# Feed-forward weights requested as one group behind a segment's output store, and GpSimd squares issued behind the values matmuls, in a segment-recurrent transformer block

## The chip, the cores and the metric

The kernel runs on one core of a Trainium2 chip. The metric is the device time of one execution in microseconds (us). Profiled executions come with a trace of every instruction and DMA packet. A profile is one execution and can lie a few us beside the median: the profiled run of the kernel before took 1187 us, 10 us over its median. So I take differences of *times* from the timed runs, and use the profiles to say *where* the time is.

## The reference, cut to what matters

```python
# 2048 rows of 640; 64 segments of 32 rows; 8 memory rows carried from segment to segment
for s in range(n_seg):
    h = concat([mem, xs])                  # 40 rows
    q, k, v = h @ Wq, h @ Wk, h @ Wv       # 32 heads of 128
    p = softmax(mask(q k^T * scale))
    o = (p v) @ Wo
    mem = o[:8]                            # the next segment needs this output
h  = x + o_all
h2 = h + relu(layernorm(h) @ w1 + b1)**2 @ w2 + b2     # feed-forward, 1728 wide
```

The recurrence over 64 segments is serial. The feed-forward part is independent work, and the kernel threads it into the recurrence: the feed-forward of one block of 128 rows is spread over four segments of the next blocks.

## The kernel before

One *segment* is one call of `step(b, sp)`, `sp` = 0 to 3. TensorE goes through: the projection passes (`ps`, 120 wide matmuls), the scores (`A`), a share of feed-forward matmuls (`psf` going up, `psy` coming down), the softmax sums (`pz`), more feed-forward, the values matmuls (`O`, 64 small ones), a strip of tail projections, and the output projection (`pw`, 128 small ones). VectorE makes `pn` = p * rz (rz, one over the softmax sums, comes from ScalarE), which the values matmuls wait for.

The feed-forward weights come from HBM in tiles of 320 KB, 14 per block, into five buffers. A tile is requested when its buffer's last matmul has been issued:

```python
def load_wf(n):
    if n < NB * FC:
        t = wfp.tile([128, 1280], BF16, tag="wf", name="wf")      # WB = 5 buffers
        nc.sync.dma_start(out=t[:], in_=wf_d[n % FC])
        wfs[n] = t
...
def run(units, us, early=False):
    while units and us > 0:
        ...
        if early and late and late[0][0]:
            late.pop(0)[1]()          # one ReLU evacuation is pulled ahead of pn
            early = False
...
# in ffn(b), up(k, u):
                if u == 1:
                    wfs.pop(b * FC + k)
                    load_wf(b * FC + k + WB)
                    late.append((1, lambda: evac(k, ps)))

        def evac(k, ps):
            r = s2.tile([128, 2, 128], BF16, tag="r", name="r")
            for u in range(2):
                nc.vector.tensor_scalar(out=r[...], in0=ps[...], ...)          # bias, ReLU
            if k < 6:
                nc.gpsimd.tensor_tensor(out=f1T[...], in0=r[:], in1=r[:], op=ALU.mult)   # square
            ...
# the feed-forward block begins with loads and a layer norm, taken one piece per projection half:
        side.append(loads)                       # x, and o back from HBM, on the Sync queue
        side.extend([lambda: None] * 3)
        side.append(add)                         # GpSimd: h = o + x
        side.extend(norm_steps(...))             # VectorE: statistics, statistics, ...
...
# in step(b, sp):
        run(full, ..., True)                     # second share of feed-forward matmuls
        ...
        nc.vector.tensor_tensor(out=pn[:, 0:MC], in0=p[:, 0:MC], in1=rz[:], op=ALU.mult)
        nc.vector.tensor_tensor(out=pn[:, MC:AC]..., in0=ptail, in1=head16(rz), op=ALU.mult)
        ... values matmuls O, evacuation oT, strip, output projection pw ...
        nc.scalar.copy(out=o[:], in_=pw[:, 0:DG])
        nc.sync.dma_start(out=o_main[b * 4 + sp]..., in_=o[:])
        ...
        run(strip, 1.28 if sp < 3 else 100)
```

After segment 0 the strip ends with the store `o_tail` of the block's last rows. `loads` (in segment 1) reads it back, so the chain `o_tail` store, `fo` load, GpSimd `add`, VectorE statistics runs through the Sync queue.

The softmax here doesn't subtract the row's maximum and nothing guards it: scores larger than these inputs give would overflow.

## Time and profile before

| | before |
|---|---|
| time, median | 1177.3 us (1173.0 to 1182.6, 20 runs) |
| profiled span, granted clock | 1185.4 us, 0.970 |
| PE / VectorE / ScalarE / GpSimd busy | 84 / 40 / 38 / 14 % |
| idle before pw matmuls, put down to "issue" | 73.2 us |
| values matmuls wait for pn | 20.6 + 9.8 us |

From the page of the kernel before: engines, the DMA queue of the instructions (packets, MB, share), the chain that ended last, and the output projection's group (busy us, mean ns | idle us before it, what ended it).

```profile
PE 994.8 (84%) x30400; PEld 727.9 (61%) x30400; DVE 477.0 (40%) x1076; ACT 449.9 (38%) x945; POOL 164.8 (14%) x468
...
q8 instruction: 237, 3.88, 1.3%
...
PE 76%; issue 8%; DMA 6%; DVE 5%; ACT 3%; POOL 1%; SPq 0%; ACTq 0%; DVEq 0%; POOLq 0%
...
L217 PE MATMUL pw<-wo,oT 128*32 128x160 bf16 x8192 | 171.6, 240 | 75.7 <-issue 73.2
```

"issue" means that TensorE waited for nothing that the profile shows. One such wait, in the timeline of TensorE before (start, us, what; in brackets the idle time before it):

```profile
535.15 1.01 PE L217 MATMUL pwt<-wo,oTt 128*32 128x160 bf16 x48
535.99 1.21 PE L217 MATMUL pw<-wo,oT 128*32 128x160 bf16 x58
539.96 1.22 PE L217 MATMUL pw<-wo,oT 128*32 128x160 bf16 x60 [2.77 <-issue]
```

The projection stops after 58 of 128 equal matmuls. Counting the TensorE instructions up to each such stop is what explains it: 49 of the 53 gaps over 0.4 us between 150 and 1095 us begin at remainder 190 modulo 256. The instruction queue q8 moves 237 packets of 16,384 bytes, and 60,800 TensorE instructions (30,400 matmuls and as many weight loads) are 237.5 times 256. So I read these as waits for the next block of 256 instructions. The packet for this stop ran from 537.63 to 538.51 us; the next matmul started 1.45 us after it.

The stretches around that stop, in the table of windows before (us, busy time of each engine, then PEclk, the granted clock, the DMA share and GB/s):

```profile
533.00:537.00 4.00, 3.45 (x186) 3.24 (x183) 3.05 (x10) 1.19 (x3) 2.48 (x9) 1.00 0.85 278
537.20:539.90 2.70, 0.00 (x0) 0.00 (x0) 0.00 (x1) 0.00 (x0) 0.46 (x2) 1.00 0.14 53
541.10:544.50 3.40, 3.35 (x102) 2.89 (x94) 0.34 (x1) 0.34 (x2) 0.00 (x0) 0.50 0.05 12
```

Just before the stop the DMA engines are 85% busy, with weight tiles. And after the stop the clock is 0.50 for 3.4 us.

The timeline before around the same segment's pn (a segment 0), where a square of GpSimd runs beside the small multiply (128x128; the large one is 128x320):

```profile
533.02 0.44 ACT L375 ACTIVATE rz<-pz 128x320 bf16<-128x320 f32 x1
...
533.69 0.32 DVE L380 TENSOR_TENSOR pn<-p,rz 128x320 bf16<-128x320 bf16 x1
...
533.85 0.62 POOL L293 TENSOR_TENSOR f1T<-r 128x256 bf16<-128x256 bf16 x1 [0.15 <-DVE r L290]
533.92 0.63 DVE L381 TENSOR_TENSOR pn<-p,rz 128x128 bf16<-128x128 bf16 x1
534.06 0.20 PE L390 MATMUL O<-pn,vr 32*128 32x40 bf16 x4 [0.20 <-DVE pn L380]
...
534.61 0.19 PE L390 MATMUL O<-pn,vt 32*128 32x16 bf16 x4 [0.35 <-DVE pn L381]
```

The multiply of 128x128 takes 0.63 us here, twice as long as the multiply of 128x320, and the values matmuls stop 0.35 us for it. Without a square beside it, it takes 0.22 us.

Three lines of the waits before (us in total, times, longest us):

```profile
PE pw L217 <- issue: 73.2, 42, 3.7
DVE lnst L117 <- POOL fx L253: 31.0, 16, 9.9
PE O L390 <- DVE pn L380: 20.6, 50, 1.4
```

### The profile page before, as it was taken

What the parts mean: (1) busy time and instruction counts of PE and PEld (TensorE: products, weight loads), DVE (VectorE), ACT (ScalarE), POOL (GpSimd) and SP (SyncE); (2) the same over time, 40 slices, a digit from 0 to 9 for tenths busy, and PEclk for the clock granted to TensorE, in tenths of its full rate; (3) what the DMA queues carried; (4) which work ended last, traced back from release to release, by engine and by line L of the source; (5) the groups of instructions that cost most, each with busy time, mean ns of one, the idle gap of its engine ahead of it and who ended that gap; (6) DMA issues with size and microseconds to landing.
All of it is one profiled execution on the core that took longest, in us unless ns stands there. A gap on an engine that the chain in (4) does not pass through costs nothing.

```text
span 1185.4 us, 64836 instructions
## 1 busy us (share of the span) xinstructions
PE 994.8 (84%) x30400; PEld 727.9 (61%) x30400; DVE 477.0 (40%) x1076; ACT 449.9 (38%) x945; POOL 164.8 (14%) x468
## 2 busy tenths in 40 slices
PE   0588798989898888998888899989988989897784
PEld 0255665666666666776666676666666766665553
DVE  0232353444444444453444445434444534453332
ACT  0234343444434433443444344334434434343320
POOL 0000101121121102011110211111021111201111
PEclk9988999999999999999999999999999999999978
DMA  9900012222132222223222222223223222322244
GB/s 388 397 12 6 23 37 71 90 88 85 57 102 88 69 90 88 75 73 96 88 69 89 88 83 73 88 88 88 71 91 99 81 60 90 95 82 71 88 149 135
DMA packets 63341, 112.61 MB, mean 95 GB/s; under 512 B 25696, under 2 KB 31968, under 8 KB 60640
## 3 DMA queue, kind: packets, MB, share of 16 engines
q1 hardware_dynamic: 61344, 96.15, 25.5%
q10 hardware_dynamic: 1728, 12.31, 2.5%
q8 instruction: 237, 3.88, 1.3%
q14 instruction: 32, 0.26, 0.1%
HBM read 102.53 MB, written 5.90 MB: 91 GB/s over the span
## 4 chain that ended last, share of the span: by engine, by line
PE 76%; issue 8%; DMA 6%; DVE 5%; ACT 3%; POOL 1%; SPq 0%; ACTq 0%; DVEq 0%; POOLq 0%
PE ps L176 35%; PE pw L217 14%; PE pst L176 9%; PE psy L309 4%; PE O L390 4%; PE pwt L217 4%; PE A L358 3%; PE psf L277 2%; DMA wo<-in_wo_dram 2%; DMA wk<-in_wk_dram 2%; DVE r L290 1%; ACT rz L375 1%; DVE pn L381 1%; DVE pn L380 1%; ACT pz L373 1%
## 5 line engine op out<-in xcount | busy, mean ns | idle before, releaser
L176 PEld LDWEIGHTS <-HT 128*32 128x32 bf16 x7680 | 257.9, 98 | 169.7 <-issue 13.1
L217 PE MATMUL pw<-wo,oT 128*32 128x160 bf16 x8192 | 171.6, 240 | 75.7 <-issue 73.2
L217 PEld LDWEIGHTS <-oT 128*32 128x32 bf16 x8192 | 154.9, 100 | 95.9 <-issue 83.0
L190 ACT CAST row<-ps 128x512 bf16<-128x512 f32 x256 | 147.9, 584 | 124.9 <-PE ps L176 124.9
L176 PE MATMUL ps<-wq,HT 128*32 128x512 bf16 x2560 | 161.5, 392 | 5.1 <-issue 2.6
L176 PE MATMUL ps<-wk,HT 128*32 128x512 bf16 x2560 | 153.9, 380 | 0.0
L176 PE MATMUL ps<-wv,HT 128*32 128x512 bf16 x2560 | 153.1, 379 | 0.0
L339 DVE STREAM_TRANSPOSE qT<-row 128x512 bf16<-128x512 bf16 x128 | 91.1, 711 | 126.8 <-ACT row L190 126.8
L339 DVE STREAM_TRANSPOSE kT<-row 128x512 bf16<-128x512 bf16 x128 | 91.0, 711 | 57.7 <-ACT row L190 57.7
L293 POOL TENSOR_TENSOR f1T<-r 128x256 bf16<-128x256 bf16 x96 | 60.1, 633 | 381.4 <-PE psf L277 195.4
L407 ACT CAST o<-pw 128x160 bf16<-128x160 f32 x64 | 18.7, 292 | 243.3 <-PE pw L217 243.3
L170 DVE STREAM_TRANSPOSE HT<-o 128x160 bf16<-128x160 bf16 x64 | 22.1, 345 | 213.0 <-ACT o L407 213.0
L400 POOL COPY oTt<-oT 128x64 bf16<-128x64 bf16 x256 | 48.9, 236 | 399.6 <-ACT oT L397 399.6
L187 ACT CAST vr<-ps 128x512 bf16<-128x512 f32 x128 | 74.9, 586 | 49.5 <-PE ps L176 49.5
L290 DVE TENSOR_SCALAR r<-psf,b1f 128x128 bf16<-128x128 f32 x224 | 67.0, 344 | 53.6 <-PE psf L277 48.6
L397 ACT CAST oT<-O 128x320 bf16<-128x320 f32 x128 | 48.2, 429 | 97.3 <-PE O L390 97.3
L309 PE MATMUL psy<-wf,f1T 128*128 128x320 bf16 x448 | 74.2, 306 | 5.7 <-DMA wf<-in_wf_dram 5.4
L399 DVE CAST oT<-O 128x320 bf16<-128x320 f32 x128 | 56.9, 486 | 52.8 <-PE O L390 52.8
L176 PEld LDWEIGHTS <-hTt 128*32 128x32 bf16 x1920 | 51.8, 99 | 41.7 <-issue 12.4
L277 PE MATMUL psf<-hnT,wf 128*128 128x128 bf16 x1120 | 74.8, 223 | 0.6 <-DVE hnT L263 0.6
L277 PEld LDWEIGHTS <-wf 128*128 128x128 bf16 x1120 | 66.0, 100 | 2.6 <-issue 0.7
L390 PE MATMUL O<-pn,vr 32*128 32x40 bf16 x2048 | 47.2, 179 | 21.0 <-DVE pn L380 20.6
(57 smaller groups left out, 1018.1 us busy)
## 6 DMA issues: line engine op xcount, KB each, us to landing
wf<-in_wf_dram SPq DMA_DIRECT2D x224, 320.0 KB
wq<-in_wq_dram ACTq DMA_DIRECT2D x3, 1024.0 KB
wk<-in_wk_dram ACTq DMA_DIRECT2D x3, 1024.0 KB
wv<-in_wv_dram ACTq DMA_DIRECT2D x3, 1024.0 KB
xt<-in_xa_dram SPq DMA_DIRECT2D x16, 160.0 KB
wo<-in_wo_dram SPq DMA_DIRECT2D x2, 1280.0 KB
wo<-in_wo_dram ACTq DMA_DIRECT2D x2, 1280.0 KB
o_main<-o SPq DMA_DIRECT2D x64, 40.0 KB
```

What stands on the lines that cost most here:

```text
L176: nc.tensor.matmul(ps[32 * g:32 * g + 32, :], lhsT=lhs(c), rhs=w[:, c, g * EG + n * 512:g * EG + (n + 1) * 512], start=(c == 0), stop=(c = ...
L187: nc.scalar.copy(out=vr[:, n * 512:(n + 1) * 512], in_=ps[:])
L190: nc.scalar.copy(out=row[:], in_=ps[:])
L217: nc.tensor.matmul(ps[32 * g:32 * g + 32, 0:DG], lhsT=lhs(s), rhs=wo[:, s, g * DG:(g + 1) * DG], start=(s == slots_all[0]), stop=(s == slo ...
L277: nc.tensor.matmul(ps[:, u * 128:(u + 1) * 128], lhsT=wfv[:, u, c], rhs=h["hnT"][:, c, :], start=(c == 0), stop=(c == DC - 1), skip_group_ ...
L290: nc.vector.tensor_scalar(out=r[0:fs, u, :], in0=ps[0:fs, u * 128:(u + 1) * 128], scalar1=b1f[0:fs, fc:fc + 1], scalar2=0.0, op0=ALU.add, ...
L293: nc.gpsimd.tensor_tensor(out=f1T[:, 2 * k:2 * k + 2, :], in0=r[:], in1=r[:], op=ALU.mult)
L309: nc.tensor.matmul(h["ps"][:, 0:320], lhsT=f1T[:, fc + i, :], rhs=wf[:, (m % 4) * 320:(m % 4 + 1) * 320], start=(fc + i == 0), stop=(fc + ...
L339: nc.vector.transpose(out=dst(n), in_=blocks(row))
L390: nc.tensor.matmul(O[c][:, i * NQ:i * NQ + n], lhsT=lhsT[r, i * 128:(i + 1) * 128], rhs=pn[r, off + i * n:off + (i + 1) * n], start=(i == ...
L399: nc.vector.tensor_copy(out=dst, in_=src)
L400: nc.gpsimd.tensor_copy(out=oTts[b][:, c * 8:(c + 1) * 8, sp * TL:(sp + 1) * TL], in_=oT[c][:, :, 0:TL])
```

## The change

The intent: keep the weight transfers out of the stretch of short matmuls, where TensorE uses up its instructions fastest (256 in some 2.4 us, against 6.9 us in the projection passes), and keep the GpSimd squares away from pn. Tiles whose buffers come free are noted and requested together right behind the segment's output store. The square of the evacuation that is pulled ahead of pn goes to the list that is worked off behind the values matmuls; its input `r` gets a third buffer for that. After the last segment (`ended`), tiles are requested at once again. Cuts in the diff are marked with three dots.

```diff
+    ended = []
+    wf_due = []
+
+    def load_due():
+        while wf_due:
+            load_wf(wf_due.pop(0))
+
+    def freed(n):
+        wf_due.append(n + WB)
+        if ended:
+            load_due()
...
             if early and late and late[0][0]:
-                late.pop(0)[1]()
+                late.pop(0)[1](True)
                 early = False
...
                     wfs.pop(b * FC + k)
-                    load_wf(b * FC + k + WB)
-                    late.append((1, lambda: evac(k, ps)))
+                    freed(b * FC + k)
+                    late.append((1, lambda *e: evac(k, ps, *e)))
...
-        def evac(k, ps):
-            r = s2.tile([128, 2, 128], BF16, tag="r", name="r")
+        def evac(k, ps, early=False):
+            r = s3.tile([128, 2, 128], BF16, tag="r", name="r")
...
+            if early:
+                late.append((0, lambda: square(k, r)))
+            else:
+                square(k, r)
+
+        def square(k, r):
             if k < 6:
                 nc.gpsimd.tensor_tensor(...)
...
                         wfs.pop(b * FC + 7 + m // 4)
-                        load_wf(b * FC + 7 + m // 4 + WB)
+                        freed(b * FC + 7 + m // 4)
...
         nc.sync.dma_start(out=o_main[b * 4 + sp].rearrange("g r d -> (g r) d"), in_=o[:])
+        load_due()
...
+    ended.append(1)
     strip.extend(wo_tail_fill(NB - 1, lambda: ffn(NB - 1)))
```

## The prediction

> **What bounds the kernel now.** TensorE: the chain of waits gives PE 76% and "issue" 8% of the span; no other engine is over 40% busy. But PE is not always fed. In the groups by line, the output-projection matmuls (pw) have 75.7 us of idle time before them, 73.2 us put down to "issue". I listed every PE gap and counted instructions: nearly all gaps over 0.5 us begin at the same place modulo 256 instructions (remainder 190). [...]queue q8 carries 237 packets of 16,384 bytes, and 60,800 PE instructions / 256 = 237.5. So these gaps are fetch stalls: 51 over 0.4 us between 150 and 1165 us, 84 us in sum.
>
> With quiet DMA: block boundary to fetch start 1.1 us, fetch 0.93, landing to first instruction 1.4, 3.45 us in all. Fast stretches (values matmuls, strip, output projection: 128 matmul pairs in some 2.4 us) are shorter, so about 1.05 us of stall stays even then. But the feed-forward weights (wf, 320 KB each, three or four per segment) are requested as buffers come free, just before this stretch, and their packets delay the fetch start to 2 to 3.6 us. Those stalls are 1.5 to 3.7 us.
>
> **Step 1, weights behind the output store.** The loads (some 3.4 us at 390 GB/s) move to the projection passes, where 128 pairs take 6.9 us, so a fetch 2.5 us late still arrives. For each stall I take off the excess over 1.1 us to the start and 0.93 us of fetch: 46 of the 84 us go, 38 stay. Five buffers hold the at most four tiles of a segment, so no matmul should wait for weights.
>
> **Step 2, squares.** Two squares per feed-forward block are "early" and move: in segments 0 and 3. There the small pn multiply takes 0.63 us against 0.22 in segments 1 and 2, because a square runs at the same time, and values matmuls span 1.16 us against 0.74. [...]Gain 0.42 us x 30 = 13 us; where the block is fetch-bound, a shorter stretch only lengthens the stall: 9 us.
>
> **What it costs.** At segment 0's end, weight loads now stand ahead of the tail store, x and o loads on one queue. The GpSimd add behind them and VectorE's statistics end with a mean slack of 1.6 us before rz (timeline); 2 to 3 us of delay makes the statistics hold pn in segment 1: about 0.4 us x 15 = 6 us. A few late fetches in the passes, and a little less clock: 4 us.
>
> **Time.** 1177 - 46 - 9 + 6 + 4 = 1132 us, range 1112 to 1155. Chance of faster by over 2%: 0.87; within 2%: 0.11; slower: 0.02.
>
> **Signs.** Right: "issue" before pw from 73 to about 30 us, remaining stalls of 1.0 to 1.1 us, none over 2; pn's small multiply at 0.22 us in all segments; values matmuls 0.74 us; pass matmuls as long as before. Wrong: stalls at pw unchanged; new gaps at pass matmuls or at A; "psy waits for wf" above 10 us; the wait for pn in segment 1 beyond 1 us.
>
> **What would make it wrong.** If the fetch delay is not due to weight traffic; if grouped loads delay fetches more than staggered ones and the passes don't hide it; if the late add delays pn by 2 us per block.

That the gaps are fetches of 256 instructions rests on the counts of the trace alone. The 390 GB/s are what the page before shows for its first two slices (388 and 397). The 4 us for late fetches and clock are an allowance; no number of a trace is under it.

## The result

| | before | after |
|---|---|---|
| time, median | 1177.3 us (20 runs) | 1140.7 us (1134.7 to 1146.3, 10 runs) |
| ratio | | 0.9684, 95% interval 0.9664 to 0.9705 |
| profiled span, granted clock | 1185.4 us, 0.970 | 1139.2 us, 0.971 |
| fetch stalls (see below): sum, number, over 1.5 us | 88.6 us, 58, 27 | 42.5 us, 52, 3 |
| small pn multiply, longest of 64 | 0.64 us | 0.22 us |
| segment 1: wait before the values matmuls | 0.37 us | 1.63 us |

A ratio is the mean time of one kernel's fast runs over that of the other's fast runs of the same rounds, so it is not quite the ratio of the medians. *Fetch stalls* in all tables from here on are TensorE gaps over 0.25 us that begin within four instructions of remainder 190 modulo 256, between the start of the second block and that of the last segment; the 84 us of the prediction used gaps over 0.4 us and a slightly different stretch. Some 36.7 us were gained of the 45 that the prediction gave. The 88.6 us come from a profile that was 10 us over its median. In the profile of shift_blocks (below; the kernel before with 32 matmuls added), 2 us over its median, the same count gives some 80 us, so up to 9 us of the 88.6 may belong to that one execution.

The page of the kernel after; its lines are 12 to 18 higher in number, L229 is the output projection:

```profile
PE 985.3 (86%) x30400; PEld 710.2 (62%) x30400; DVE 462.8 (41%) x1076; ACT 449.8 (39%) x945; POOL 160.9 (14%) x468
...
PE 69%; DMA 14%; issue 7%; DVE 3%; POOL 3%; ACT 3%; SPq 1%; POOLq 0%; DVEq 0%; ACTq 0%
...
L229 PE MATMUL pw<-wo,oT 128*32 128x160 bf16 x8192 | 175.4, 245 | 28.4 <-issue 26.0
```

The wait for issue in front of pw fell by 47 us, and the chain now holds 14% of DMA against 6%. The waits after say where that comes from:

```profile
DVE lnst L129 <- POOL fx L265: 75.1, 16, 10.3
...
PE O L408 <- DVE pn L398: 38.6, 49, 3.2
...
PE pw L229 <- issue: 26.0, 33, 1.6
```

VectorE's statistics wait 44 us longer for GpSimd's add, and the values matmuls wait 18 us longer for the large pn multiply. Means of the trace over all segments from the second block on, in us, show that both are one matter, in segment 1:

| | segment 0 | segment 1 | segment 2 | segment 3 |
|---|---|---|---|---|
| whole segment, before | 18.68 | 16.10 | 16.80 | 16.84 |
| whole segment, after | 17.06 | **17.50** | 15.27 | 15.49 |
| end of A to the values matmuls, before | 2.71 | 2.50 | 2.51 | 2.57 |
| end of A to the values matmuls, after | 2.68 | **3.76** | 2.51 | 2.53 |
| values matmuls, before / after | 1.15 / 0.74 | 0.74 / 0.75 | 0.74 / 0.74 | 1.13 / 0.74 |
| values matmuls' end to pw's end, before / after | 5.62 / 4.35 | 4.12 / 4.22 | 4.71 / 3.64 | 4.21 / 3.65 |

Three segments became faster by 1.3 to 1.6 us, and segment 1 slower by 1.4. One such segment 1 in the timeline after, from the output store of the segment before it:

```profile
328.83 0.33 SPq L426 DMA_DIRECT2D o_main<-o  x1
...
329.25 2.84 SPq L95 DMA_DIRECT2D wf<-in_wf_dram  x4
...
332.14 0.42 SPq L246 DMA_DIRECT2D o_tail<-ot  x1
...
338.53 0.31 SPq L261 DMA_DIRECT2D fo<-o_tail  x1
...
339.02 0.44 ACT L393 ACTIVATE rz<-pz 128x320 bf16<-128x320 f32 x1
...
340.59 1.39 POOL L265 TENSOR_TENSOR fx<-fo,fx 128x640 bf16<-128x640 bf16 x1 [13.38 <-issue]
342.01 0.49 DVE L129 BATCH_NORM_STATS2 lnst<-fx 128x6 f32<-128x320 bf16 x1 [6.48 <-POOL fx L265]
342.42 0.31 DVE L398 TENSOR_TENSOR pn<-p,rz 128x320 bf16<-128x320 bf16 x1
...
342.79 0.20 PE L408 MATMUL O<-pn,vr 32*128 32x40 bf16 x4 [3.22 <-DVE pn L398]
```

Read it from the bottom. The values matmuls waited 3.22 us for pn. Its input rz was complete at 339.46, but pn started at 342.42, behind the statistics, which stand before it in VectorE's order and waited for GpSimd's add. The add waited for the load of the tail rows, which was issued at 338.53, more than 6 us after the store that it reads back. And that store stood behind four weight tiles. As means over 14 blocks, counted from the o_main store: the last `fo` load is issued 5.17 us after it before and 8.47 after; the statistics end at 9.56 and 12.85; rz ends at 11.22 and 11.41.

### The profile page after: what moved, and what is told of

It is laid out like the page before. It is cut to its first block, busy times and chain, and to the rows that moved or that the text cites. A ratio compares the mean times of both kernels' runs of the same rounds, so it can differ in the third digit from the quotient of the medians.

```text
span 1139.2 us, 64855 instructions
## 1 busy us (share of the span) xinstructions
PE 985.3 (86%) x30400; PEld 710.2 (62%) x30400; DVE 462.8 (41%) x1076; ACT 449.8 (39%) x945; POOL 160.9 (14%) x468
## 4 chain that ended last, share of the span: by engine, by line
PE 69%; DMA 14%; issue 7%; DVE 3%; POOL 3%; ACT 3%; SPq 1%; POOLq 0%; DVEq 0%; ACTq 0%
PE ps L188 29%; PE pw L229 14%; PE pst L188 10%; DMA o_tail<-ot 6%; PE O L408 4%; PE pwt L229 3%; PE psy L327 3%; DMA fo<-o_tail 3%; PE A L376 2%; PE psf L289 2%; DMA wo<-in_wo_dram 2%; POOL fx L265 2%; DMA wk<-in_wk_dram 2%; DVE r L302 1%; DMA wf<-in_wf_dram 1%
## 5 line engine op out<-in xcount | busy, mean ns | idle before, releaser
L188 PEld LDWEIGHTS <-HT 128*32 128x32 bf16 x7680 | 240.8, 97 | 177.4 <-issue 6.3
L229 PE MATMUL pw<-wo,oT 128*32 128x160 bf16 x8192 | 175.4, 245 | 28.4 <-issue 26.0
L229 PEld LDWEIGHTS <-oT 128*32 128x32 bf16 x8192 | 161.4, 103 | 47.9 <-issue 35.0
L188 PE MATMUL ps<-wq,HT 128*32 128x512 bf16 x2560 | 152.4, 379 | 4.2 <-DVE HT L182 2.3
L311 POOL TENSOR_TENSOR f1T<-r 128x256 bf16<-128x256 bf16 x96 | 57.4, 612 | 334.9 <-DVE r L302 169.2
L188 PEld LDWEIGHTS <-hTt 128*32 128x32 bf16 x1920 | 49.3, 99 | 38.2 <-issue 9.1
L408 PEld LDWEIGHTS <-vr 32*128 32x128 bf16 x2048 | 42.3, 92 | 47.2 <-issue 40.7
```

The lines of the kernel that those rows point to most:

```text
L188: nc.tensor.matmul(ps[32 * g:32 * g + 32, :], lhsT=lhs(c), rhs=w[:, c, g * EG + n * 512:g * EG + (n + 1) * 512], start=(c == 0), stop=(c = ...
L229: nc.tensor.matmul(ps[32 * g:32 * g + 32, 0:DG], lhsT=lhs(s), rhs=wo[:, s, g * DG:(g + 1) * DG], start=(s == slots_all[0]), stop=(s == slo ...
L311: nc.gpsimd.tensor_tensor(out=f1T[:, 2 * k:2 * k + 2, :], in0=r[:], in1=r[:], op=ALU.mult)
L408: nc.tensor.matmul(O[c][:, i * NQ:i * NQ + n], lhsT=lhsT[r, i * 128:(i + 1) * 128], rhs=pn[r, off + i * n:off + (i + 1) * n], start=(i == ...
```

## The experiments

All ratios below are against runs of the kernel before on the same chip (median 1175.6 to 1176.6 us). All runs were fast, but for one of the four of shift_blocks and one of the seven beside it. "Right result" means that the outputs agreed with the reference.

### loads_only: the grouped requests without the moved squares

```diff
 (against after)
-                late.pop(0)[1](True)
+                late.pop(0)[1]()
...
-            if early:
-                late.append((0, lambda: square(k, r)))
-            else:
-                square(k, r)
+            square(k, r)
```

The evacuation's `r` comes from two buffers again, as before.

> The change without its part about the squares. Theory: the fetch stalls fall from 84 to about 40 us (-46) and the late add costs 22 us (segment 1 waits 1.65 us for pn instead of 0.30), so the time is about 1177 - 46 + 22 = 1153 us, 11 to 14 us above the whole change; values matmuls keep a span of 1.16 us in segments 0 and 3. Rival (the squares, not the loads, bring most of the gain): above 1165 us, with stalls at pw as before.

Measured: right result, 1149.6 us, ratio 0.9778 (0.974 to 0.9816). This is faster beyond noise; whether by more than 2% is left open by the interval. Fetch stalls 40.7 us, none over 1.5 us; segment 1 waits 1.66 us; the values matmuls span 1.13 us in segments 0 and 3. The rival falls: the loads bring the gain and the new wait both, and the squares on top of them bring 9 us (1149.6 to 1140.7; the two ratios give 11 us, each known to some 4 us).

### squares_only: the moved squares without the grouped requests

```diff
 (against after)
-        wf_due.append(n + WB)
-        if ended:
-            load_due()
+        load_wf(n + WB)
```

> The change without its part about the loads. Theory: the small pn multiply takes 0.22 us and the values matmuls 0.74 us in all segments, 13 us less, of which some is given back as longer fetch stalls (sum of stalls from 84 up to about 88): 1164 to 1170 us. Segment 1 waits for pn as before, 0.30 us. Rival (nothing given back): 1164 us and the stalls at 84. Rival (the squares are worth nothing by themselves): 1177 us.

Measured: right result, 1175.4 us, ratio 0.9982 (0.9945 to 1.0019): no gain that can be told from noise, where I had expected 7 to 13 us. The mechanism is there: the values matmuls span 0.74 us in every segment. But in segment 0 the stretch from their end to the end of pw grew from 5.62 to 6.07 us, as much as was gained in front of it. The sum of fetch stalls is 88.6 us as before, and 11 windows of half clock stand against 9. The gain of segment 3 (0.39 us in the values matmuls) was not given back there: that segment fell from 16.84 to 16.16 us. The two profiles are 10 us apart (1185.4 and 1175.4 us) where the timed runs are 0 to 2 us apart, since the profile of the kernel before was a long one. So the giving back is seen in segment 0 and not shown as a sum; where the rest of the gain went stays open.

### no_weights: the kernel before without weight traffic (a wrong result)

```diff
 (against before)
-        if n < NB * FC:
+        if n < WB:
...
-            wfs[n] = t
+            for m in range(n, NB * FC, WB):
+                wfs[m] = t
```

> The kernel before, with only the first five weight tiles ever loaded and used again and again (a wrong result on purpose): no weight traffic at all, everything else as before. Theory (weight packets delay the instruction fetches): the stalls fall to the floor that I reckoned, about 38 us, and the time to about 1131 us; what remains are stalls of 1.0 to 1.1 us at the same instruction count modulo 256. Rival (fetches are slow by themselves, the weights are innocent): stalls stay near 84 us and the time near 1177 us.

Measured: wrong result, 1109.9 us, ratio 0.9444 (0.9404 to 0.9484). Fetch stalls 41.1 us, three over 1.5 us. This settles the mechanism: with no weights in flight the long stalls are gone, and the floor is the same 40 to 47 us that the grouped requests reach (40.7 us in loads_only). The idle time in the waits of this kernel:

```profile
PE pw L218 <- issue: 28.2, 38, 1.6
```

The time is 21 us below what I expected. 13 of them lie in the tail of the program after the last segment begins (43.7 us against 56.6), which I did not take apart. The clock is a likely part of the other 8 us, which no run here splits up: no half-clock window is left in its main part (150 us to the last segment), against 30.7 us before. See the experiments on idle time.

The 41.1 us that remain stand at block boundaries too. Medians over the stalled blocks of this run: from the start of the block that TensorE works through to the start of the packet for the next one 1.03 us (0.6 to 1.6), the packet 1.13, from its landing to the first instruction 1.37, 3.5 us in sum, while TensorE got through those blocks in 2.6 us. With weights in flight, in the kernel before, the packet started up to 3.65 us after the start of the block, and the stall was up to 3.73 us.

### shift_blocks: all instructions moved 64 places on

```diff
 (against before)
+    pd = mm.tile([128, 512], F32, tag="mm", name="pd")
+    for i in range(32):
+        nc.tensor.matmul(pd[:, 0:128], lhsT=ident, rhs=ident, start=True, stop=True)
```

> The kernel before with 32 extra small matmuls (64 TensorE instructions, about 2 us) at the very start, so that all later instructions stand 64 places further on in the blocks of 256. Theory (the stalls sit at block boundaries of the instruction fetch): counted over all TensorE instructions the long stalls begin again at remainder 190, so counted in the program's own instructions at 126, elsewhere in the output projection or another group than before; their number and sum stay alike, 75 to 95 us, and the time within 1165 to 1190 us. Rival (the stalls belong to places in the program, such as a certain matmul of the output projection that waits for something unseen): they stay at 190 of the program's own count, 254 of the whole.

Measured: right result, 1171.9 us (four runs, one of them slow, at 1189.1; the fast ones 1168.5 to 1173.5), ratio 0.996 (0.9871 to 1.005). Of 58 gaps over 0.4 us, 51 begin at remainder 190 of all TensorE instructions, which is 126 of the program's own; before it was 49 of 53 at 190. Their sum is 76.3 us against 80.4. The stalls belong to the count of instructions and not to places in the program.

### stats_later: the new wait taken away

```diff
 (against after)
-        side.extend([lambda: None] * 3)
+        side.extend([lambda: None] * 5)
```

Two more empty places put the add and the statistics into segment 2. The order of all DMA requests stays that of the change.

> The whole change, with two more empty places ahead of the GpSimd add of x and o, so that add and statistics fall into segment 2 and VectorE has no statistics in front of pn in segment 1. The DMA order is the changed one. Theory (the new wait is VectorE's in-order queue, held by statistics that wait for the late add): segment 1 waits for pn about 0.3 us instead of 1.65, 18 to 22 us less than the changed kernel, 1119 to 1124 us. Rival (late transfers disturb segment 1 in another way, by DMA traffic or by fetches): the time stays at 1140 us, and the wait moves to another line.

Measured: right result, **1115.9 us** (1112.1 to 1120.2), ratio 0.9487 (0.9455 to 0.952). It beats both kernels, by 60 and 25 us. The waits of it:

```profile
PE pw L229 <- issue: 28.8, 38, 1.6
...
PE O L408 <- DVE pn L398: 20.0, 50, 1.4
...
DVE lnst L129 <- POOL fx L265: 9.3, 1, 9.3
```

The wait for pn is back at the 20 us of before, segment 1 takes 15.86 us, and the fetch stalls stay low (47.0 us). So the new wait was VectorE's order, and no other loss from the late transfers can be seen in segment 1 (15.86 us against 16.10 before). It gained 25 us where the wait itself is worth about 19 (15 segments x 1.26 us). In segment 1 the stretch from the values matmuls to the end of pw also fell, from 4.22 to 3.72 us, which is 7.5 us over 15 segments. All half-clock time of the changed kernel's main part stood in segment 1 (27.3 us) and is gone here; the experiments on idle time show the connection.

### tail_first: the same wait, attacked through the queue

```diff
 (against after)
-        load_due()
+        if sp > 0 or b == 0:
+            load_due()
...
                               in_=o_tail[b].rearrange("g r d -> r g d"))
+            load_due()                      # at the end of loads()
```

> The whole change, but after segment 0 the weight requests stand behind the tail store and the loads of x and o instead of in front of them; GpSimd's add and the statistics stay where the change has them. Theory (the add is late because its loads queue behind 1.28 MB of weights): the last o load is issued about 5 us after the o_main store again instead of 8 to 9, and segment 1 waits for pn at most about 0.4 us instead of 1.65; but the weights of segment 0 now travel some 4 us later, close to the fast stretch of segment 1, which may bring back a few fetch stalls or a wait for weights there: 1118 to 1132 us. Rival (the delay of the add has nothing to do with the order of the requests): 1140 us with the wait unchanged.

Measured: right result, 1129.8 us, ratio 0.9605 (0.957 to 0.964). The last o load is issued 5.43 us after the o_main store (5.17 before, 8.47 after), and segment 1 waits for pn 0.12 us. The order of requests on the queue is therefore the cause of the late load, and with the add left in its place, of the late add. But another wait comes instead:

```profile
PE psy L328 <- DMA wf<-in_wf_dram: 12.7, 18, 1.3
```

The downward matmuls, mostly those of segment 1, now wait for their weights (2.9 us in the changed kernel), and its stretch from A to the values matmuls is 3.10 us against 2.50 in stats_later. Here, moving the user of the late data (1115.9 us) was better than moving the transfers.

### later_no_squares: what the squares are worth with fetches on time

This is loads_only with the two extra empty places of stats_later.

> The statistics_later kernel with the squares put back where they were. It asks what the squares are worth once long fetch delays are gone, against nearly nothing (2 us) when they were moved alone. Theory (moved alone, their gain in segment 0 came back as longer fetch stalls there; here the fetches are on time): 9 to 13 us slower than stats_later, 1125 to 1129 us. Rival (moving the squares is worth nothing anywhere): 1116 us.

Measured: right result, 1123.8 us, ratio 0.9572 (0.9533 to 0.9612). The squares are worth 8 us here by the medians and 10 by the ratios (each ratio known to some 4 us), near the low end of what I expected, and 9 us on top of loads_only, against 0 to 2 alone. With the long fetch stalls gone, their gain shows. The runs compared here come from separate calls, each beside the kernel before.

### idle_short and idle_long: TensorE idle for 1.1 and 2.75 us per block

```diff
 (against stats_later; n = 2 for idle_short, 5 for idle_long)
+        if sp == 2:
+            for _ in range(n):
+                nc.vector.transpose(out=pn[:, 0:MC], in_=rz[:])      # overwritten by pn
```

> The statistics_later kernel with two extra VectorE transposes of 128x320 ahead of pn in segment 2 of each of the 16 blocks, overwritten afterwards (right result): TensorE idles there about 1.0 us more. Theory[...] (only gaps of about 2 us or more are followed by 3.4 us at half clock): no more half-clock windows than in stats_later (7), about 16 us slower: 1128 to 1134 us. Rival (every idle time costs clock): more windows in proportion.

> The same with five extra transposes, about 2.6 us idle in each block. Theory[...]: after most of the 16 gaps a window of 3.4 us at half clock shows, each costing up to 1.7 us more: 41 us of idle plus 15 to 27 us of clock, 1170 to 1184 us. Rival (no clock effect of gaps): 1157 us and 7 windows.

Measured: right results. idle_short 1136.8 us, ratio 0.9666 (0.9623 to 0.971); idle_long 1176.5 us, ratio 1.001 (0.9956 to 1.0063). Against stats_later that is 20.8 and 60.6 us. The windows around one gap of idle_short:

```profile
616.20:617.20 1.00, 0.00 (x0) 0.00 (x0) 0.93 (x4) 0.00 (x0) 0.00 (x0) 1.00 0.00 0
617.50:620.90 3.40, 3.40 (x198) 2.94 (x200) 1.69 (x4) 0.75 (x2) 1.10 (x5) 1.00 0.15 50
```

and of idle_long:

```profile
639.50:642.10 2.60, 0.00 (x0) 0.00 (x0) 2.43 (x7) 0.00 (x0) 0.00 (x0) 1.00 0.00 0
643.30:646.70 3.40, 3.40 (x96) 2.93 (x92) 1.38 (x4) 0.46 (x2) 1.10 (x5) 0.51 0.16 53
```

In the profile before, the half-clock time of the main part comes in nine windows of 3.41 us, and 8 of the 14 fetch stalls over 2 us were followed by one. After the long gap here, 3.4 us pass at clock 0.51; after the short gap the clock stays at 1.00. (The two windows begin at different distances from their gaps, so their counts of matmuls can't be compared.) In idle_long all 15 gaps of over 2.5 us are followed by such a window; in idle_short none of the 28 of 1.0 to 1.5 us. In segment 2 of idle_long, the wait before the values matmuls grew by 2.73 us and the stretch behind them by another 1.35 us (4.91 against 3.56): that is the clock's share. idle_short came out 3 us slower than my range; the wait grew by 1.09 us in each of 16 blocks, which explains 17 of the 20.8 us; the other 3 us stay unexplained. (The 7 windows in the expectation count the whole execution of stats_later, its start and tail too; idle_short has 8 by the same count.)

Over all profiles but shift_blocks, in the main part of the program:

| idle gap of TensorE | gaps | followed by 3.4 us or more at half clock |
|---|---|---|
| 1.0 to 1.5 us | 168 | 2 |
| 1.5 to 2.0 us | 55 | 6 |
| 2.0 to 2.5 us | 13 | 7 |
| 2.5 to 3.0 us | 26 | 24 |
| over 3.0 us | 14 | 11 |

And the half-clock time in the main part of each: before 30.7 us, squares_only 41.0, after 27.3, loads_only 20.5, stats_later 0, no_weights 0. A window of 3.4 us at half clock costs about 1.7 us of work, an estimate from its length and the clock. The time lost can be less. In segment 1 of the changed kernel, the 8 windows went with 7.5 us and not with 13.6; the fetch stalls of that segment sum to 5.5 us there and to 8.8 us in stats_later, so shorter stalls hide a part of it.

## Why the prediction was right, and where a term was off

The prediction of 1132 us (1112 to 1155) against 1140.7 measured holds, and the mechanism of its main gain holds. Its signs were mixed. Of those for "right", the wait for issue before pw fell from 73.2 to 26.0 us, no stall over 2 us is left (14 before), and the small multiply and the values matmuls take 0.22 and 0.74 us in all segments. One of those for "wrong" came true: the wait for pn in segment 1 is 1.63 us, where I had set the limit at 1 us. Step by step,

- **The gaps at pw are instruction fetches, lengthened by weight packets.** Shown: shift_blocks moved them with the instruction count, no_weights and loads_only took the long ones away. Predicted "46 of the 84 us go, 38 stay"; by the table's count 46 of 88.6 went and 42.5 stayed. The counts fit 256 instructions to a packet of queue q8: 237 packets of 16,384 bytes for 60,800 TensorE instructions.
- **The passes hide the weights.** Shown: the pass matmuls have a median of 379 ns before and after, "psy waits for wf" is 2.9 us.
- **Squares, 9 us.** Right on top of the loads (9 us, and 8 in later_no_squares). I had reckoned with some gain lost where a stretch is bound by fetches; moved alone, the squares lost nearly all of it (0 to 2 us gained). The small multiply takes 0.22 us in every segment, against 0.63 with a square beside it. The runs show the overlap and the slowing, not what in the hardware causes it.
- **The term that was mis-sized: "about 0.4 us x 15 = 6 us" for the late add.** It measured 1.26 us x 15 = 19 us. The statistics came 3.3 us later (9.56 to 12.85 us after the o_main store) where I had reckoned "2 to 3 us". My own terms, 2 to 3 us of delay less 1.6 us of slack, give 0.4 to 1.4 us, and I took the lower end; the measured ones are 3.3 - 1.7 = 1.6 us, of which 1.26 shows as added wait. What I had not worked through is that the tail store and the load that reads it are two trips in series and the store lands only behind the weights: from its issue to the issue of the last load it is 3.0 us before and 5.6 after. tail_first shows that the order of the requests is the cause: the order alone brought the last load back from 8.47 to 5.43 us after the o_main store.
- **The term that was missing: the clock.** I had set down "a little less clock". In truth 8 of the 14 fetch stalls over 2 us had been paid twice, by the stall and by 3.4 us of half clock behind it. Taking them away could win up to some 15 us more, an estimate from half of the 30.7 us. The changed kernel did not collect it: the gaps of 1.7 to 3.2 us in its own segment 1 brought half-clock windows back (27.3 us). stats_later has no half-clock window left in its main part; how much of the 15 us it collected, no run separates.

In sum, with the timed runs: the loads without the new wait and without the squares win 52 us (later_no_squares); the squares win 8 more (stats_later); the late add takes 25 back, 19 as waiting; the rest fits the 7.5 us in segment 1 that went with the half clock. That leaves 35, and the whole change measured 36.7. That the prediction came within 9 us of the time is in part luck: the loads won 52 us where I had 46, the 4 us that I set down for late fetches and clock were not seen as a loss, and the late add took 25 where I had 6. These errors partly cancel.

## What to carry to other kernels

When TensorE stops in the middle of equal matmuls with nothing to wait for, count its instructions modulo 256 (here 49 of 53 such gaps began at one remainder) and look which transfers are in flight. Bulk transfers belong into stretches where one block of instructions lasts longer than a fetch with traffic: here a block lasts 6.9 us in the passes, and the latest fetch in the main part of the profile before (the stop at 296.9 us) took 5.9 us from the start of the block before it to the next matmul (3.65 to the start of the packet, 0.92 of packet, 1.36 to the matmul). When requests are regrouped on a queue, follow every short round trip that shares this queue (here the last `fo` load came 3.3 us later) through to the engine that uses its result in program order (here pn started 2.96 us after rz was complete, behind the statistics), and move that user away from the critical chain. And a TensorE gap over 2 us can cost more than its length: here 42 of 53 such gaps were followed by half clock.
